# Turning the normalized rows of h with VectorE and small transfers instead of TensorE

## The chip, the cores and the metric

The kernel runs on one core of a Trainium2 chip. The metric is the device time of one execution in microseconds, and every comparison is between executions on the same chip. Engines are named as in the profile: PE (TensorE matmuls), PEld (its weight loads), DVE (VectorE), ACT (ScalarE), POOL (GpSimd) and SP (SyncE, which here only issues transfers).

## The reference

One transformer block on x of 2048 rows and 512 columns, float32: attention with 32 heads of 16, then a gated MLP whose gate mixes rows.

```python
q, k, v = split((layernorm(x) @ wqkv))           # 32 heads of 16
h = x + softmax(q k^T / 4) v @ wo                # 2048 x 512
z = gelu(layernorm(h) @ w_in)                    # 2048 x 1376
z1, z2 = z[:, :688], layernorm(z[:, 688:])
g = w_sp @ z2 + b_sp[:, None]                    # w_sp is 2048 x 2048
out = h + (z1 * g) @ w_out
```

## The kernel before

The program has four stages: projections of x; attention; a middle stage that turns each block of 128 rows of attention output into h, normalizes it and multiplies it into z; and the products with w_sp and w_out. Float32 operands of matmuls are split into a high and a low part (hi, lo), and a product is three matmuls (`mm3`, lines 108 to 110). The split is a copy by ACT into a rounded type (hi) and a subtraction by DVE (lo), line 100 and line 105.

The middle stage (lines 1000 to 1110) runs over 16 row blocks in the order of `h_rows`; step k finishes block `row[k]` and begins block `row[k + 3]`. PE, ACT, DVE, POOL and SP each work strictly in the order in which the program issues instructions there, so what stands behind a waiting instruction waits too. In step k:

- `make_h` (line 643): 12 matmuls of the split o with wo give h of `row[k + 3]`; DVE adds x (line 653), SP stores h to the scratch `h_scr` (line 655), and DVE takes its statistics (line 657) and computes mean and 1/std by small operations (lines 119 to 135).
- `turn` (line 1015): PE transposes the four 128x128 pieces of hn, the normalized block, of `row[k + 1]` into a PSUM tile, and ACT and DVE split them into hT.
- `make_z` on three groups of columns (464, 448, 464): 12 matmuls each, then gelu by ACT (line 1034). Between the first and the second group ACT and DVE split the o of `row[k + 4]` (`split_o`, lines 100 and 105, with the tile named o); after the second, DVE takes statistics of z (line 1094) and ACT writes hn of `row[k + 3]` (line 1097).
- `gate_z`: ACT's queue stores z (lines 1041 and 1047), ACT normalizes z2 (line 1046), and `load_o` fetches what `row[k + 5]` needs: o from its scratch (line 623), the reciprocal softmax sums rc, each row of which is read by 16 partitions (four transfers, line 626), and x (line 629). POOL then multiplies o by rc (line 630). In the second half POOL also forms sums of z for the next stage.

The last three steps make no h. The first three blocks are made at the end of attention (`more_h`, line 863): their matmuls stand among those of attention by the string FINAL, and DVE writes hn (line 883). The line 195 loads v in pieces of 128 bytes during attention; lines 285 and 677 are small transfers there.

Of the kernel before, what the change touches and what calls it, by code (L numbers as in the profile page):

```python
# [20 lines left out]
D = 512  # L21
# [5 lines left out]
NB = S // P  # L27
HB = NB // 2
NQ = S // 512
DB = D // P  # L30
# [30 lines left out]
def block_kernel(ctx: ExitStack, tc: tile.TileContext, x, wqkv, wo, w_in, w_sp4, b_sp, w_out, out):  # L61
# [7 lines left out]
    nc = tc.nc  # L69
# [20 lines left out]
    o_scr = dram.tile([D, S], F32, name="o_scr")  # L90
    r_scr = dram.tile([H, S], F32, name="r_scr")
    h_scr = dram.tile([S, D], F32, name="h_scr")
    z_scr = [dram.tile([S, FH], F32, name=f"z{i}_scr") for i in range(2)]
    s_scr = dram.tile([HB, P, HB, P], F32, name="s_scr")
    g_scr = [dram.tile([3, P, FC], F32, name=f"g{p}_scr") for p in range(HB)]

    def split(hi, lo, src, eh=None, el=None):

        if eh == "act":
            nc.scalar.activation(hi, src, AF.Copy)  # L100
        elif eh == "pool":
            nc.gpsimd.tensor_copy(hi, src)  # L102
        else:
            nc.vector.tensor_copy(hi, src)
        (nc.gpsimd if el == "pool" else nc.vector).tensor_sub(lo, src, hi.bitcast(F32))
# [508 lines left out]
    wi4 = w_in.rearrange("(a p) c -> p a c", p=P)  # L614

    h_rows = [0, 1, 2, HB, HB + 1, HB + 2] + [sb + HB * i for sb in range(3, HB) for i in range(2)]
    os_, o2s, xrs, hns, hTs = {}, {}, {}, {}, {}

    def load_o(sb):

        c = slice(sb * P, (sb + 1) * P)
        o = e2.tile([P, DB, P], F32, name="o")
        nc.sync.dma_start(o, o_scr[:, c].rearrange("(d p) s -> p d s", p=P))
        rc = e2.tile([P, DB, P], F32, name="rc")
        for d in range(DB):
            nc.sync.dma_start(rc[:, d, :], r_scr[8 * d:8 * d + 8, c].rearrange(
                "h (o s) -> h o s", o=1).to_broadcast([8, DH, P]))
        xrs[sb] = e2.tile([P, D], F32, name="xr", bufs=3)
        nc.sync.dma_start(xrs[sb], x[c, :])
        nc.gpsimd.tensor_mul(o, o, rc)  # L630
        os_[sb] = o
# [19 lines left out]
    def add_h(sb, acc, between=lambda: None):  # L651
        h = xrs[sb]
        nc.vector.tensor_add(h, acc, h)
        between()
        nc.sync.dma_start(h_scr[sb * P:(sb + 1) * P, :], h)
        hst[sb] = e2.tile([P, 6], F32, name="st")
        nc.vector.bn_stats(hst[sb], h)

    def scale_h(sb):
        mv = e2.tile([P, 2], F32, name="mv")  # L660
# [21 lines left out]
    with ExitStack() as at:  # L682
# [127 lines left out]
        def play_final(units):  # L810


            half = []
            for x in FINAL:
                if x == "G":
                    if not half:
                        unit = units.pop(0)
                        half.extend([unit, new_pt(), 0])
                        if unit[2] == 6 and sums_:
                            invert()  # L820
                        if len(units) in (7, 5):
                            load_o(h_rows[(7, 5).index(len(units)) + 3])
                    unit, pt, p = half
                    for step in score(unit, p, pt):
                        step()
                    half[2] += 1
                    if p:
                        waiting.append([(unit, pt, PLACES), 0])
                        half.clear()
                elif x == "V":  # L830
                    unit, *rest = waiting.pop(0)[0]
                    weigh(unit, *rest)
                    if unit[2] == NB - 1:
# [29 lines left out]
        def more_h(k):  # L863

            for _ in range(k):
                if not pieces:
                    sb = h_rows[len(hns)]
# [8 lines left out]
                after = h_rows[len(hns) + 1]  # L876
                o = os_.pop(after)
                hi, lo = o2s[after] = [e2.tile([P, DB, P], F32R, name=f"o2{i}", bufs=1) for i in range(2)]
                nc.vector.tensor_copy(hi, o)
                add_h(sb, acc, lambda: nc.vector.tensor_sub(lo, o, hi.bitcast(F32)))  # L880
                mv, rs = scale_h(sb)
                hns[sb] = e2.tile([P, D], F32, name="hn", bufs=3)
                nc.vector.tensor_scalar(hns[sb], xrs.pop(sb), mv[:, 0:1], rs,
                                        op0=ALU.subtract, op1=ALU.mult)

        made = [0]
        units = [(hg, qb, kb) for hg in range(HG) for qb in range(NQ) for kb in range(NB)]
# [3 lines left out]
        with tc.manual_schedule(engines={E.PE, E.Activation, E.DVE, E.SP}):  # L891
            end = len(units) - 2 * LEAD
            for n in range(0, end, 2):
                hg, qb, kb = units[n]
                if hg + 1 < HG and n % 64 < 24 and n % 4 == 0:
                    load_k(hg + 1, [n % 64 // 4])
                if hg + 1 < HG and n % 64 < 12 and n % 4 == 2:
                    load_d(hg + 1, [n % 64 // 4])
                if hg + 1 < HG and n % 64 == 30:
                    load_v(hg + 1)  # L900
                if kb == 2 and n // NB + 3 < HG * NQ:
                    load_q(n // NB + 3)
# [18 lines left out]
            load_o(h_rows[2])  # L921
            maxima.close()
# [77 lines left out]
    with ExitStack() as mid:  # L1000
        m2 = mid.enter_context(tc.tile_pool(name="mid_2", bufs=2))
        zs, zst = {}, {}
        hT = wc.tile([P, 2, 2, DB, P], F32R, name="hT", tag="w2")
        ph = mid.enter_context(tc.tile_pool(name="mid_ph", bufs=1, space=PSUM))
        pt = mid.enter_context(tc.tile_pool(name="mid_pt", bufs=2, space=PSUM))
        ps = mid.enter_context(tc.tile_pool(name="mid_ps", bufs=5, space=PSUM))

        turned = [0]

        def turn(sb):  # L1010

            hn = hns.pop(sb)
            tp = pt.tile([P, DB, P], F32, name="tp")
            for d in range(DB):
                nc.tensor.transpose(tp[:, d, :], hn[:, d * P:(d + 1) * P], ident)  # L1015
            hTs[sb] = [hT[:, i, turned[0] % 2] for i in range(2)]
            turned[0] += 1
            split(hTs[sb][0], hTs[sb][1], tp, "act")

        def new_z(sb):  # L1020
            zs[sb] = [m2.tile([P, FH], F32, name=f"z{i}", bufs=1 + 4 * i) for i in range(2)]
# [45 lines left out]

        w = [Slot(wc, f"w{i}") for i in range(3)]
        row = dict(enumerate(h_rows))
        turn(row[0])  # L1070
        for k in range(NB):
            sb, new = row[k], row.get(k + 3)
            if new is not None:
                make_h(new, (ph if k else ps).tile([P, 512], F32, name="acc"))
            if k + 1 < NB:
                turn(row[k + 1])
            if new is not None:
                mv, rs = scale_h(new)
                nb = minus_mean(e2, mv, rs)
# [13 lines left out]
            for c in range(2):  # L1093
                nc.vector.bn_stats(zst[sb][:, c, :], zs[sb][1][:, c * FC:(c + 1) * FC])
            if new is not None:
                hns[new] = e2.tile([P, D], F32, name="hn", bufs=3)
                nc.scalar.activation(hns[new], xrs.pop(new), AF.Identity, bias=nb, scale=rs)
            for c in chunks[2:]:
                make_z(sb, *c)
            hTs.pop(sb)  # L1100
# [358 lines left out]
```

## Time and profile before

| | |
|---|---|
| median of 3 runs | 1803.24 us (1802.75 to 1803.64) |
| profiled execution | 1802.38 us |
| its span in the profile | 1800.6 us |
| busy share of PE, DVE, ACT, POOL | 100%, 83%, 77%, 12% |
| middle stage | about 1351 to 1514 us |
| transfers of SP's queue | 143224 packets, 143.82 MB |

Rows of a timeline are start, duration (both us), engine, line, operation, output and input, and in brackets the engine's idle time before it with what ended it. SPq and ACTq are the queues of SP and ACT that issue transfers; the duration is that of the issue, not of the transfer. A row "x4" merges neighbours of one kind. Rows of a group have the median in the middle of three durations, in ns. The chain is the work that ended last, followed back from the end.

### The profile page before, as it was taken

The numbers are of one execution on the slowest core, as the hardware profiler recorded it, in microseconds if no ns is written. First come the engines' busy times: TensorE is split into PE (matmuls) and PEld (weight loads), VectorE is DVE, ScalarE is ACT, GpSimd is POOL, SyncE is SP. The second block draws the span as 40 slices with busy tenths as digits, with TensorE's granted clock in tenths as the row PEclk, the third lists the DMA queues.
The fourth block names the chain that finished last, engine by engine and source line by source line (L and its number), as shares of the span: only waits on it lengthen the run. The fifth ranks groups of instructions, "written<-read, shape, count | busy, mean of one in ns | idle before, by whom it ended". The sixth has DMA issues, their size and how long they took to land.

```text
span 1800.6 us, 36057 instructions
## 1 busy us (share of the span) xinstructions
PE 1793.1 (100%) x13371; PEld 1050.6 (58%) x13371; DVE 1500.0 (83%) x3034; ACT 1378.4 (77%) x2674; POOL 218.4 (12%) x299
## 2 busy tenths in 40 slices
PE   9999999999999999999999999999999999999999
PEld 6876444444444444444444444444448889999998
DVE  6487999999999999999999999999936676778664
ACT  3224999999999999999999999999994445334231
POOL 2241000011010100000000000000110754001111
PEclk9999999999999999999999999999999999999999
DMA  6677111221120111021012011100134554668562
GB/s 199 192 194 182 43 26 27 49 56 30 36 59 19 51 39 26 20 50 35 14 36 44 24 30 38 26 15 15 40 74 143 168 176 151 216 208 278 184 197 91
DMA packets 148184, 157.54 MB, mean 87 GB/s; under 512 B 63032, under 2 KB 93256, under 8 KB 146664
## 3 DMA queue, kind: packets, MB, share of 16 engines
q1 hardware_dynamic: 143224, 143.82, 29.6%
q10 hardware_dynamic: 4752, 11.41, 1.6%
q8 instruction: 105, 1.72, 0.4%
q14 instruction: 71, 0.58, 0.1%
q0 software_dynamic: 32, 0.01, 0.0%
HBM read 99.69 MB, written 54.56 MB: 86 GB/s over the span
## 4 chain that ended last, share of the span: by engine, by line
PE 99%; DVE 1%; DMA 0%; issue 0%; ACT 0%; DVEq 0%
PE pv L726 30%; PE s L700 10%; PE s L237 9%; PE m L700 9%; PE m L237 7%; PE acc L108 6%; PE acc L110 6%; PE acc L109 6%; PE g L110 4%; PE g L109 4%; PE g L108 4%; PE acc L643 2%; PE tp L1319 1%; PE h L643 1%; PE acc L1340 0%; PE tp L1015 0%
## 5 line engine op out<-in xcount | busy, mean ns | idle before, releaser
L704 ACT ACTIVATE pt<-s 128x512 f32<-128x512 f32 (+1 forms) x1149 | 668.5, 632 | 3.4 <-PE s L700 3.0
L726 PE MATMUL pv<-pt,vst 128*32 128x256 f32 (+1 forms) x6048 | 595.2, 467 | 0.0
L242 DVE TENSOR_REDUCE mx<-s 128x1 f32<-128x512 f32 x826 | 539.6, 682 | 42.3 <-PE s L237 34.4
L704 ACT ACTIVATE pt<-m 128x512 f32<-128x512 f32 x855 | 500.3, 616 | 0.2 <-PE m L700 0.2
L242 DVE TENSOR_REDUCE mx<-m 128x1 f32<-128x512 f32 x682 | 452.3, 682 | 28.3 <-PE m L237 21.2
L700 PE MATMUL s<-qst,kst 50*128 50x512 f32 x1193 | 418.5, 437 | 0.0
L237 PE MATMUL s<-kst,qst 48*128 48x512 f32 x963 | 343.7, 421 | 0.0
L700 PE MATMUL m<-qst,kst 50*128 50x512 f32 x855 | 340.1, 440 | 0.0
L237 PE MATMUL m<-kst,qst 48*128 48x512 f32 x794 | 290.8, 423 | 0.0
L700 PEld LDWEIGHTS s<-qst,kst 50*128 50x128 f32 x1193 | 187.4, 184 | 145.0 <-DVE mx L242 91.0
L726 PEld LDWEIGHTS pv<-pt,vst 128*32 128x32 f32 x6048 | 120.4, 108 | 217.6 <-issue 208.5
L700 PEld LDWEIGHTS m<-qst,kst 50*128 50x128 f32 x855 | 146.2, 184 | 129.4 <-DVE mx L242 88.9
L237 PEld LDWEIGHTS s<-kst,qst 48*128 48x128 f32 x963 | 166.8, 184 | 40.4 <-issue 12.8
L237 PEld LDWEIGHTS m<-kst,qst 48*128 48x128 f32 x794 | 137.1, 184 | 41.7 <-issue 15.2
L247 ACT ACTIVATE ab<-s 128x512 f32<-128x512 f32 x167 | 100.4, 601 | 14.2
L102 POOL CAST mparts<-nm 128x16 fp32r<-128x16 f32 x32 | 6.3, 196 | 861.3 <-DVE nm L255 861.3
L251 DVE CUSTOM_DVE_ANT_0 ab<-s,ab 128x512 f32<-128x512 f32 x137 | 93.2, 680 | 5.1 <-PE s L237 5.1
L955 ACT ACTIVATE ws<-a 128x512 fp32r<-128x512 f32 x80 | 45.7, 621 | 48.7 <-PE g L110 23.8
L251 DVE CUSTOM_DVE_ANT_0 ab<-m,ab 128x512 f32<-128x512 f32 x112 | 76.2, 680 | 4.9 <-PE m L237 4.9
L237 PE MATMUL s<-dst,qst 48*128 48x512 f32 x167 | 79.6, 477 | 0.0
L1034 ACT ACTIVATE z<-acc 128x464 f32<-128x464 f32 (+2 forms) x64 | 27.5, 456 | 63.5 <-PE acc L110 63.5
L108 PE MATMUL acc<-wi,hT 128*128 128x464 f32 (+2 forms) x196 | 72.8, 371 | 0.0
(219 smaller groups left out, 2586.9 us busy)
## 6 DMA issues: line engine op xcount, KB each, us to landing
a<-in_w_sp SPq DMA_DIRECT2D x80, 256.0 KB
qst<-q_scr SPq DMA_DIRECT2D x192, 64.0 KB
z_scr<-z ACTq DMA_DIRECT2D x32, 344.0 KB
kst<-k_scr SPq DMA_DIRECT2D x42, 256.0 KB
k_scr<-part SPq DMA_DIRECT2D x16, 512.0 KB
q_scr<-part SPq DMA_DIRECT2D x16, 512.0 KB
z<-z_scr SPq DMA_DIRECT2D x14, 344.0 KB
b<-z_scr SPq DMA_DIRECT2D x24, 172.0 KB
```

The source lines that it names most:

```text
L108: nc.tensor.matmul(ps, lh, rh, start=first, stop=False)
L109: nc.tensor.matmul(ps, lh, rl, start=False, stop=False)
L110: nc.tensor.matmul(ps, ll, rh, start=False, stop=last)
L237: nc.tensor.matmul(acc, q[r, p, c], keys[r, p], start=True, stop=True)
L242: nc.vector.reduce_max(at(t, e if t else e - 1), acc, axis=AX.X)
L247: nc.scalar.activation(ab[0], acc, AF.Relu)
L251: nc.vector.tensor_tensor_reduce(ab[0], acc, ab[0], 1.0, LOW, ALU.add, ALU.max, at(0, 0))
L643: yield nc.tensor.matmul(acc, o2[b][:, d, :], wo2[a][:, d, :], start=i == 0, stop=i == 3 * DB - 1)
L700: nc.tensor.matmul(out, kst[hg % 2][r, p, kb * P:(kb + 1) * P], qst[hg * NQ + qb][r, p, :], start=True, stop=True)
L704: nc.scalar.activation(out, scores, AF.Exp, scale=DH ** -0.5)
L726: nc.tensor.matmul(pv[0][32 * j:32 * j + 32, cols], vst[hg % 2][:, c:c + 32], pt[:, places[t, p], cols], start=kb == 0, stop=kb == NB - 1 ...
L955: nc.scalar.activation(hi, src, AF.Copy)
```

## The change

The transposes of hn by PE go, with the PSUM tile they used. Instead, as soon as hn is written, `flip` has DVE transpose the block in 32x32 squares, each in its place, and four transfers of SP (512 pieces of 128 bytes each) carry the squares to their transposed places in a new scratch in DRAM, `ht_scr`. A step later `fetch_turned` loads the turned block (256 KB) from there, and a step after that `split_turned` has ACT and DVE split it, now from SBUF. The first block is fetched and split during the end of attention, by DVE alone, and the second is fetched there.

```diff
+    def flip(sb, hn):
+        z = e2.tile([P, D], F32, name="hz", tag="hn", bufs=3)
+        nc.vector.transpose(z, hn)
+        q = 32
+        for i in range(P // q):
+            c = sb * P + q * i
+            nc.sync.dma_start(ht_scr[:, c:c + q].rearrange("(j r) c -> r j c", r=q),
+                              z[q * i:q * i + q, :].rearrange("r (j c) -> r j c", c=q))
+
+    def fetch_turned(sb, pool, **slot):
+        raws[sb] = pool.tile([P, DB, P], F32, name="ht", **slot)
+        nc.sync.dma_start(raws[sb], ht_scr[:, sb * P:(sb + 1) * P].rearrange("(a p) s -> p a s", p=P))
+
+    def split_turned(sb, eh=None):
+        hTs[sb] = [hT[0][:, i, turns[0] % 2] for i in range(2)]
+        turns[0] += 1
+        split(hTs[sb][0], hTs[sb][1], raws.pop(sb), eh)
...
@@ play_final, more_h: the end of attention
+                        if len(units) in (13, 3):
+                            fetch_turned(h_rows[(13, 3).index(len(units))], e2, tag="rc")
...
+                if made[0] == 6 * DB:
+                    split_turned(h_rows[0])
...
+                flip(sb, hn)
@@ the middle stage
-        pt = mid.enter_context(tc.tile_pool(name="mid_pt", bufs=2, space=PSUM))
-        ps = mid.enter_context(tc.tile_pool(name="mid_ps", bufs=5, space=PSUM))
-        def turn(sb):
-            hn = hns.pop(sb)
-            tp = pt.tile([P, DB, P], F32, name="tp")
-            for d in range(DB):
-                nc.tensor.transpose(tp[:, d, :], hn[:, d * P:(d + 1) * P], ident)
...
-            split(hTs[sb][0], hTs[sb][1], tp, "act")
+        ps = mid.enter_context(tc.tile_pool(name="mid_ps", bufs=7, space=PSUM))
...
-        turn(row[0])
         for k in range(NB):
...
             if k + 1 < NB:
-                turn(row[k + 1])
+                split_turned(row[k + 1], "act")
+            if k + 2 < NB:
+                fetch_turned(row[k + 2], m2)
...
             if new is not None:
-                hns[new] = e2.tile([P, D], F32, name="hn", bufs=3)
-                nc.scalar.activation(hns[new], xrs.pop(new), AF.Identity, bias=nb, scale=rs)
+                hn = e2.tile([P, D], F32, name="hn", bufs=3)
+                nc.scalar.activation(hn, xrs.pop(new), AF.Identity, bias=nb, scale=rs)
+                flip(new, hn)
             for c in chunks[2:]:
                 make_z(sb, *c)
             hTs.pop(sb)
             gate_z(sb, lambda: k + 5 < NB and load_o(row[k + 5]))
```

SP in one step of the middle stage, before, from one store of h to the next (xr holds h here, and then x of a later block):

```order
L655 DMA h_scr<-xr 128x512
L623 DMA o<-o_scr 128x4x128
L626 DMA rc<-r_scr 128x1x128 x4
L629 DMA xr<-in_x 128x512
L655 DMA h_scr<-xr 128x512
```

and after (lines 656, 624, 627 and 630 are the old 655, 623, 626 and 629):

```order
L656 DMA h_scr<-xr 128x512
L673 DMA ht<-ht_scr 128x4x128
L667 DMA ht_scr<-hz 32x16x32 x4
L624 DMA o<-o_scr 128x4x128
L627 DMA rc<-r_scr 128x1x128 x4
L630 DMA xr<-in_x 128x512
L656 DMA h_scr<-xr 128x512
```

The load of a turned block and the four transfers to the scratch now stand between the store of h and the six transfers of load_o.

DVE in the same step, before, around the statistics of z (o is the low part of the split o):

```order
L666 TENSOR_SCALAR nb<-rs_r_19272,mv 128x1
L105 TENSOR_TENSOR o_19294<-o,o_19293 128x512
L1094 BN_STATS zst<-z_19277 128x6 x2
L1043 BN_AGGR zmv<-zst 128x2
L119 TENSOR_SCALAR rs_v_19333<-zmv 128x1
```

and after:

```order
L690 TENSOR_SCALAR nb<-rs_r_19287,mv 128x1
L106 TENSOR_TENSOR o_19309<-o,o_19308 128x512
L1111 BN_STATS zst<-z_19292 128x6 x2
L663 STREAM_TRANSPOSE hz<-hn 128x512
L1059 BN_AGGR zmv<-zst 128x2
L120 TENSOR_SCALAR rs_v_19354<-zmv 128x1
```

The transpose stands behind the statistics of z and ahead of the operations that make its mean and 1/std. ACT's order is as it was, but for the source of the split into hT.

More of the change, by code (lines that the diff above doesn't have):

```diff
@@ L92, in block_kernel @@
     h_scr = dram.tile([S, D], F32, name="h_scr")
+    ht_scr = dram.tile([D, S], F32, name="ht_scr")
     z_scr = [dram.tile([S, FH], F32, name=f"z{i}_scr") for i in range(2)]
@@ L616, in block_kernel @@
     h_rows = [0, 1, 2, HB, HB + 1, HB + 2] + [sb + HB * i for sb in range(3, HB) for i in range(2)]
-    os_, o2s, xrs, hns, hTs = {}, {}, {}, {}, {}
+    os_, o2s, xrs, hTs = {}, {}, {}, {}
     def load_o(sb):
@@ L657, in add_h @@
         nc.vector.bn_stats(hst[sb], h)
+    def flip(sb, hn):
[13 more added lines that the diff above has]
+        split(hTs[sb][0], hTs[sb][1], raws.pop(sb), eh)
+    raws, turns, hT = {}, [0], []
     def scale_h(sb):
@@ L866, in more_h @@
                 if not pieces:
-                    sb = h_rows[len(hns)]
+                    sb = h_rows[made[0] // (3 * DB)]
                     acc = later[0].tile([P, 512], F32, name="h")
@@ L875, in more_h @@
                 pieces.clear()
-                after = h_rows[len(hns) + 1]
+                if made[0] == 6 * DB:
+                    split_turned(h_rows[0])
+                after = h_rows[made[0] // (3 * DB)]
                 o = os_.pop(after)
@@ L881, in more_h @@
                 mv, rs = scale_h(sb)
-                hns[sb] = e2.tile([P, D], F32, name="hn", bufs=3)
-                nc.vector.tensor_scalar(hns[sb], xrs.pop(sb), mv[:, 0:1], rs,
+                hn = e2.tile([P, D], F32, name="hn", bufs=3)
+                nc.vector.tensor_scalar(hn, xrs.pop(sb), mv[:, 0:1], rs,
                                         op0=ALU.subtract, op1=ALU.mult)
+                flip(sb, hn)
         made = [0]
@@ L921, in block_kernel @@
             load_o(h_rows[2])
+            hT.append(wc.tile([P, 2, 2, DB, P], F32R, name="hT", tag="w2"))
             maxima.close()
@@ L1095, in block_kernel @@
             if new is not None:
-                hns[new] = e2.tile([P, D], F32, name="hn", bufs=3)
-                nc.scalar.activation(hns[new], xrs.pop(new), AF.Identity, bias=nb, scale=rs)
+                hn = e2.tile([P, D], F32, name="hn", bufs=3)
+                nc.scalar.activation(hn, xrs.pop(new), AF.Identity, bias=nb, scale=rs)
+                flip(new, hn)
             for c in chunks[2:]:
```

4 lines of the change are left out of this document (removed).

## Prediction

> **What bounds the kernel now.** I read the page first, then stretches of the stage that turns hn into z (about 1351 to 1514 us), then the chain through that stage, then the waits.
>
> ```profile
> PE 1793.1 (100%) x13371; PEld 1050.6 (58%) x13371; DVE 1500.0 (83%) x3034; ACT 1378.4 (77%) x2674; POOL 218.4 (12%) x299
> PEclk9999999999999999999999999999999999999999
> ```
>
> PE has no idle time worth the name and the granted clock is full in every slice, so time can only be won by giving PE less, and is lost as soon as PE waits. The stretches of the stage (busy us of PE, PEld, DVE, ACT, POOL; then clock, DMA share, GB/s), with the end of attention first:
>
> ```profile
> 1300.00:1351.00 51.00, 50.98 (x362) 20.72 (x358) 20.42 (x57) 47.86 (x58) 5.82 (x6) 1.00 0.29 67
> 1362.00:1426.00 64.00, 64.00 (x314) 56.34 (x313) 44.75 (x146) 27.14 (x48) 32.02 (x37) 1.00 0.57 170
> 1426.00:1512.00 86.00, 86.00 (x432) 76.75 (x431) 55.91 (x180) 37.25 (x67) 55.98 (x65) 1.00 0.53 166
> ```
>
> PE is busy for all of it; ACT has half its time free, DVE a third, the DMA engines over 40%. Now the chain over the stage, and over one step of its loop:
>
> ```profile
> by line: PE acc L110 24.4%; PE acc L109 24.3%; PE acc L108 24.3%; PE acc L643 22.0%; PE tp L1015 4.4%; PE pv L726 0.3%; PE g L108 0.2%; PE g L110 0.2%; PE g L109 0.2%
> ```
> ```profile
> 1383.99 2.76 PE acc L643 x12
> 1386.75 0.44 PE tp L1015 x4
> ```
> ```profile
> 1351.36 0.59 PE tp L1015 x4
> ...
> 1394.66 2.77 PE acc L643 x12
> ```
>
> The chain is PE alone. A step with an h takes 1394.66 - 1383.99 = 10.67 us; the turning by TensorE that the change removes is 0.44 us of it (0.59 for the first), and 4.4% of 163.7 us = 7.2 us in all. That is the whole prize: without it a step is 10.23 us.
>
> **The change part by part.** *Removed:* 64 transposes, 7.2 us of PE, all of it on the chain. ACT and DVE split as many elements as before, from SBUF instead of PSUM: nothing, they have room.
>
> *Added:* per row block one 128x512 transpose on DVE, four transfers of 512 pieces of 128 bytes on SP, and one load of the turned block. What matters is where they stand. On SP the four transfers stand ahead of the six transfers of load_o, and they wait for hn, which ACT makes only after its split of o in the same step. Load_o fetches the o that ACT splits in the next step. So a ring closes: split of o, two gelus, hn (ACT), transpose (DVE), four transfers, load_o (SP), landing, o times rc (POOL), the next split of o. One turn of the ring is one step. In the kernel before, load_o stood right behind the store of h, early in the step, and no such ring existed:
>
> ```profile
> 1387.51 0.33 SPq L655 DMA_DIRECT2D h_scr<-xr  x1
> 1387.93 0.39 SPq L623 DMA_DIRECT2D o<-o_scr  x1
> 1388.37 2.47 SPq L626 DMA_DIRECT2D rc<-r_scr  x4
> ...
> 1390.94 0.39 SPq L629 DMA_DIRECT2D xr<-in_x  x1
> ```
>
> Its time round is a sum of rows. ACT and DVE first, in step 0, where nothing waits between them:
>
> ```profile
> 1359.52 0.62 ACT L100 ACTIVATE o<-o 128x512 fp32r<-128x512 f32 x1
> 1360.17 0.61 ACT L1034 ACTIVATE z<-acc 128x224 f32<-128x224 f32 x2
> 1360.66 0.82 ACT L1097 ACTIVATE hn<-xr,nb,rs_r 128x512 f32<-128x512 f32 x1
> ```
> ```profile
> 1346.76 0.43 DVE L879 CAST o<-o 128x512 fp32r<-128x512 f32 x1 [7.72 <-PE h L643]
> ...
> 1350.99 0.55 DVE L883 TENSOR_SCALAR hn<-xr,mv,rs_r 128x512 f32<-128x512 f32 x1
> ...
> 1360.18 0.69 DVE L105 TENSOR_TENSOR o<-o,o 128x512 fp32r<-128x512 f32 x1 [1.32 <-ACT o L100]
> 1360.79 0.93 DVE L1094 BATCH_NORM_STATS2 zst<-z 128x6 f32<-128x344 f32 x2
> ```
> ```profile
> L281 DVE STREAM_TRANSPOSE mturned<-mparts x32: 199/204/211, 142.7 to 1307.2; 128x32 f32<-128x32 f32 x32
> ```
>
> Hn ends 1360.66 + 0.82 - 1359.52 = 1.96 us after the split of o starts, but DVE, which has the transpose behind the statistics of z, is free at 1360.79 + 0.93 - 1359.52 = **2.20**. The only transpose in the trace has 32 columns (0.20 us); for 512 columns the other operations of that shape take 0.43 to 0.69. I take **0.7**, with 0.43 below and 1.1 (twice 0.55) above.
>
> Then SP's issuing, and how long load_o takes to be usable:
>
> ```profile
> 1304.82 0.38 SPq L623 DMA_DIRECT2D o<-o_scr  x1
> ...
> 1327.99 1.70 SPq L677 DMA_DIRECT2D r_scr<-rcp  x4
> ...
> 1368.13 0.47 SPq L623 DMA_DIRECT2D o<-o_scr  x1
> ```
> ```profile
> L285 SPq DMA_DIRECT2D qst<-mturned x256: 610/610/1058, 143.0 to 1313.4; - x128
> ```
> ```profile
> 1312.64 1.29 POOL L630 TENSOR_TENSOR o<-o,rc 128x512 f32<-128x512 f32 x1 [5.48 <-DMA rc<-r_scr]
> ...
> 1377.81 1.29 POOL L630 TENSOR_TENSOR o<-o,rc 128x512 f32<-128x512 f32 x1 [8.69 <-DMA rc<-r_scr]
> ...
> 1396.52 1.28 POOL L630 TENSOR_TENSOR o<-o,rc 128x512 f32<-128x512 f32 x1 [9.46 <-DMA rc<-r_scr]
> ```
>
> Four small transfers in a row cost SP 1.70 us (r_scr) to 4 x 0.61 = 2.44 (mturned): **2.1**. From the issue of load_o's first transfer to POOL's start on it: 1396.52 - 1387.93 = 8.59 in a mid step, 1377.81 - 1368.13 = 9.68 in another, and 1312.64 - 1304.82 = 7.82 at the end of attention, before any z or h store adds traffic. So it is the load's own time, not a queue: **8.6**. POOL's product: **1.3**. Sum: 2.2 + 0.7 + 2.1 + 8.6 + 1.3, and 0.1 for the handing over, is **15.0 us** a turn, against 10.23 that PE would need. The ring, not PE, sets the step.
>
> What the 2048 new packets of a step take on the DMA engines is not in the trace as a write. The nearest row is the load of v, which moves 4096 pieces of 128 bytes:
>
> ```profile
> 236.59 2.18 SPq L195 DMA_DIRECT2D raw<-v_scr  x2
> ```
> ```profile
> 237.00:242.00 5.00, 5.00 (x43) 2.35 (x43) 4.68 (x10) 4.95 (x12) 0.00 (x0) 1.00 0.73 110
> ```
>
> 0.73 x 5.0 us x 16 engines / 4096 = 14 ns a piece, so 2048 take 1.8 us of all engines. They pass while SP issues (2.1 us), so I add 0; at worst load_o queues behind all 1.8. Ends of the turn: 2.20 + 0.43 + 1.70 + 7.82 + 1.28 = 13.4 below, 2.20 + 1.1 + 2.44 + 9.68 + 1.29 + 1.8 = 18.5 above. [...]
>
> *How the ring adds up.* Load_o runs in steps 0 to 10, so there are 11 turns between the split of o in step 0 and in step 11:
>
> ```profile
> 1475.62 0.62 ACT L100 ACTIVATE o<-o 128x512 fp32r<-128x512 f32 x1
> ```
> ```profile
> 1476.27 0.69 DVE L105 TENSOR_TENSOR o<-o,o 128x512 fp32r<-128x512 f32 x1
> ```
> ```profile
> 1479.91 2.93 PE L643 MATMUL acc<-wo,o 128*128 128x512 f32 x12
> ```
>
> The first split moves up by the two turnings ahead of it, 0.59 + 0.44: 1359.52 - 1.03 = 1358.5. Eleven turns of 15.0 put the last at 1523.5 (now 1475.62). Both halves of o are ready 1476.27 + 0.69 - 1475.62 = 1.34 later; PE starts the last h at 1524.8 instead of 1479.91: 44.9 late. After it three turnings are still saved, 3 x 0.44 = 1.3. Net **+43.6 us**. Break-even is a turn of 11.0 us: 1358.5 + 11 x 11.03 + 1.34 - 1.3 is 1479.9.
>
> *What I cost at nothing.* The three blocks turned during attention: DVE is busy for 20 of 51 us there, SP's later transfers move by 2.1 us, and r_scr, written last, is read steps later. The DVE transpose delays the statistics chain of z by 0.7 us; ACT waits there with nothing due. The loads of turned blocks are issued a step before they are split. For the last one the time is shortest:
>
> ```profile
> 1482.84 0.44 PE tp L1015 x4
> ...
> 1490.76 0.44 PE tp L1015 x4
> ```
>
> Steps without h take 7.92 - 0.44 = 7.5 us, so from hn in step 12 (some 9 us into it) to its product in step 15 there are 10.2 + 7.5 + 7.5 - 9 = 16 us, for 0.7 + 2.1 and twice a landing of up to 5: covered by 3 us; it would show only if both landings took over 6.6.
>
> Idle PE of 15.0 - 10.2 = 4.8 us a step is new; the trace, at full clock throughout, cannot show what follows an idle. [...]
>
> **The rivals.**
> *The ring is hidden, and PE's saving is all that shows.* If load_o were usable 3.8 us after its issue, a turn would be 10.2 and PE would stay the bound: 1802.4 - 7.2 = 1795.2. For it: in mid steps the load shares the engines with stores, so its 8.6 us could shrink at the new place. Against it: 7.82 at a quiet time. The decision falls at a turn of 10.23.
> *The load is quicker, but not by that much.* At a turn near 11.0 nothing changes: 1802. It needs the load in 4.6 us.
> *The small writes are dear.* If each of the 2048 packets took what the mean packet of SP's queue takes,
>
> ```profile
> q1 hardware_dynamic: 143224, 143.82, 29.6%
> ```
>
> 0.296 x 1800.6 us x 16 / 143224 = 59.5 ns, a block needs 128 x 59.5 ns = 7.6 us on each engine; load_o queues behind 7.6 - 2.1 = 5.5 of it, a turn is 20.5, and the kernel takes 1846 + 11 x 5.5 = 1906.5. For it: they are scattered writes to DRAM. Against it: 14 ns apiece in reads of the same size. [...]
>
> **How the numbers follow.** The profiled execution took 1802.38 us (its span 1800.6), 0.05% under the median of the runs, 1803.24; sums are against it, and a shift of 0.9 is within what I can tell. A measurement can tell about 0.2% (3.6 us) from no change. Forecast 1802.4 + 43.6 = **1846.0**, chance 0.82, from 1828.7 (turn 13.4) to 1884.6 (turn 18.5). Hidden ring 0.07 (1795.2), no change 0.03, dear writes 0.08 (1906.5). Since the five terms will not all be at one end, 1827 to 1878 holds 8 in 10. Faster 0.07, same 0.03, slower 0.90.
>
> **What would show it.** Right: no TensorE transposes in this stage; PE idle before L643 in steps 1 to 12, ended by the split of o; ACT's split of o waiting for POOL, POOL for rc; SP waiting for the transpose ahead of the four transfers; h stores about 15 us apart, then steps of 10.2 and 7.5. Wrong: h stores 10.2 us apart, or PE waiting for the turned block's split (then the round trip through the scratch is the bound), or load_o landing in under 5 us.

## The result, and the profile after

| | before | after |
|---|---|---|
| median of 6 runs | 1802.95 us (1802.62 to 1803.64) | 1861.73 us (1858.83 to 1863.08) |
| ratio | | 1.0323 [1.0310, 1.0336] |
| profiled execution | 1802.38 us | 1859.43 us |
| its span | 1800.6 us | 1857.6 us |

The changed kernel is 3.2% slower. First PE and its granted clock on the page, and the middle stage in the two stretches shown of before (busy us of PE, PEld, DVE, ACT, POOL; then clock, DMA share, GB/s):

```profile
PE 1807.0 (97%) x13307; PEld 1053.1 (57%) x13307; DVE 1513.7 (81%) x3051; ACT 1376.9 (74%) x2673; POOL 221.5 (12%) x299
PEclk9999999999999999999999999999998899999999
```
```profile
1362.00:1426.00 64.00, 47.59 (x196) 39.09 (x197) 33.12 (x105) 20.96 (x39) 7.39 (x7) 0.89 0.53 147
1426.00:1512.00 86.00, 69.16 (x282) 57.28 (x282) 46.03 (x147) 24.06 (x43) 42.86 (x51) 0.88 0.57 149
```

PE, busy for all of both stretches before, is now idle for 16 of 64 us and 17 of 86, and the clock, full before, is at 0.88 to 0.89. No other engine got busier: something waits, nothing is overloaded. The waits of the stage (engine, line, what it waited for: total us, times, longest) name the chain:

```profile
POOL o L631 <- DMA rc<-r_scr: 102.2, 11, 14.8
ACT o L101 <- POOL o L631: 79.3, 11, 8.6
PE acc L644 <- ACT o L101: 42.4, 12, 5.2
```

PE waits for ACT's split of o, ACT for POOL's product, POOL for the reciprocal sums. One turn, on the chain from one split of o to the next (which began at 1393.94 and begins again at 1408.05):

```profile
1396.14 0.61 DVE hz L663
...
1397.15 0.54 SPq L667
...
1399.10 0.45 SPq L624
1399.60 0.59 SPq L627
...
1401.48 5.15 DMA rc<-r_scr
...
1406.75 1.27 POOL o L631
...
1408.05 0.64 ACT o L101
```

This is the ring of the prediction: transpose, four transfers, load_o, landing, product, split. It is 14.11 us here. ACT's first operations of the stage, and its last split of o:

```profile
1361.48 1.28 ACT L1050 ACT_TABLE_LOAD   x1 [8.07 <-DMA sums<-o]
...
1363.23 0.62 ACT L101 ACTIVATE o<-o 128x512 fp32r<-128x512 f32 x1
```
```profile
1533.43 0.63 ACT L101 ACTIVATE o<-o 128x512 fp32r<-128x512 f32 x1 [8.15 <-POOL o L631]
```

Eleven turns lie between, so a mean turn is (1533.43 - 1363.23) / 11 = 15.47 us, against 15.0 forecast. PE's first matmuls of an h in a mid step, of the last h, and the first product with w_sp:

```profile
1394.62 4.73 PE L644 MATMUL acc<-wo,o 128*128 128x512 f32 x12 [5.24 <-ACT o L101]
```
```profile
1534.12 1.55 PE L644 MATMUL acc<-wo,o 128*128 128x512 f32 x3 [4.49 <-ACT o L101]
```
```profile
1569.57 0.40 PE L109 MATMUL g<-t,ws 128*128 128x344 f32 x1 [0.59 <-POOL t L986]
```

The last h starts 54.2 us later than before (1479.91), and the execution ends 57.05 us later (1859.43 - 1802.38). The first split of o is only 3.7 us later than before (1363.23 against 1359.52), so 50.5 us of the loss lie inside the ring.

### The profile page after: what moved, and what is told of

The parts are those of the page before. It is cut to its first block, busy times and chain, and to the rows that moved or that the text cites. A ratio compares the mean times of both kernels' runs of the same rounds, so it can differ in the third digit from the quotient of the medians.

```text
span 1857.6 us, 36087 instructions
## 1 busy us (share of the span) xinstructions
PE 1807.0 (97%) x13307; PEld 1053.1 (57%) x13307; DVE 1513.7 (81%) x3051; ACT 1376.9 (74%) x2673; POOL 221.5 (12%) x299
## 4 chain that ended last, share of the span: by engine, by line
PE 87%; DMA 5%; DVE 3%; SPq 3%; ACT 1%; POOL 1%; issue 1%; POOLq 0%; ACTq 0%; DVEq 0%
PE pv L750 29%; PE s L724 10%; PE s L238 9%; PE m L724 8%; PE m L238 7%; PE g L111 4%; PE g L110 4%; PE g L109 4%; DMA rc<-r_scr 4%; PE acc L109 3%; PE acc L111 3%; PE acc L110 3%; SPq L667 1%; SPq L627 1%; POOL o L631 1%
## 5 line engine op out<-in xcount | busy, mean ns | idle before, releaser
L248 ACT ACTIVATE ab<-s 128x512 f32<-128x512 f32 x167 | 100.5, 602 | 14.1
L644 PE MATMUL acc<-wo,o 128*128 128x512 f32 x156 | 55.2, 514 | 42.5 <-ACT o L101 42.4
```

The costliest lines, as they stand in the source:

```text
L248: nc.scalar.activation(ab[0], acc, AF.Relu)
L644: yield nc.tensor.matmul(acc, o2[b][:, d, :], wo2[a][:, d, :], start=i == 0, stop=i == 3 * DB - 1)
```

## The experiments

The theory from the profile: the four transfers stand ahead of load_o on SP and close a ring; without that the change would cost nothing. Rivals: the 128-byte pieces are dear in themselves; or the load's landing is set by other traffic. Each ratio below is to the kernel before on the same chip.

**The prize alone.** The kernel before without the transposes of PE:

```diff
...
-            tp = pt.tile([P, DB, P], F32, name="tp")
-            for d in range(DB):
-                nc.tensor.transpose(tp[:, d, :], hn[:, d * P:(d + 1) * P], ident)
+            tp = hn.rearrange("p (d s) -> p d s", d=DB)
```

> The kernel before with the transposes by TensorE left out: hn is split into hT as it stands, so h is not turned and z is of other numbers. It measures the prize alone. All theories: 7.2 us of PE's chain go, 1795 to 1797 us. If PE's own time were not the bound of the stage, 1800 or more.

Measured: 1797.88 us (1797.35 to 1798.94), ratio 0.9971 [0.9960, 0.9982]. What PE can give back is about 5 us, a little less than the 7.2 read off the chain.

**One store ahead of load_o.** No small piece anywhere, the kernel before with one plain store of hn on SP:

```diff
...
                 nc.scalar.activation(hns[new], xrs.pop(new), AF.Identity, bias=nb, scale=rs)
+                nc.sync.dma_start(hn_scr[new * P:(new + 1) * P, :], hns[new])
```

> The kernel before, turning by TensorE, with one plain store of hn (256 KB in rows of 2 KB, to a scratch that nobody reads) issued on SP ahead of load_o. No small pieces, no transpose on DVE, no round trip. Theory (ring): the wait of that one transfer for hn closes the same ring with a shorter turn: 1.96 (split to hn) + 0.5 (issue) + 7.7 to 8.6 (load_o) + 1.3 (POOL) + 0.1 = 11.6 to 12.5 us against a step of 10.67, so 1811 to 1822 us. Rivals 1 and 2: nothing of theirs is in it, 1803 to 1805 us.

Measured: 1832.10 us (1829.56 to 1835.89), ratio 1.0163 [1.0146, 1.0180]; a turn of 13.31 us. SP's and ACT's waits of this kernel between 1362 and 1512 us:

```profile
SPq L1099 <- ACT hn L1098: 81.4, 11, 8.7
```
```profile
ACT o L101 <- POOL o L631: 55.3, 11, 6.3
```

A single plain store costs 1.6% when it waits for hn ahead of load_o. The ring needs neither small pieces nor VectorE. It costs more than I expected because load_o, started there, took 9.2 to 10.3 us to reach POOL.

**Large pieces.** The changed kernel, the same four transfers, in pieces of 512 bytes:

```diff
-            c = sb * P + q * i
-            nc.sync.dma_start(ht_scr[:, c:c + q].rearrange("(j r) c -> r j c", r=q),
-                              z[q * i:q * i + q, :].rearrange("r (j c) -> r j c", c=q))
+            c = sb * P
+            nc.sync.dma_start(ht_scr[P * i:P * i + P, c:c + P].rearrange("(r j) c -> r j c", j=DB),
+                              z[q * i:q * i + q, :].rearrange("r (j c) -> r j c", c=P))
```

> The changed kernel with the same four transfers, same bytes and same place in SP's order, but in 512 pieces of 512 bytes a block instead of 2048 of 128 bytes; the squares are then not put in their places, so the block isn't turned. Theory (ring): SP still issues four transfers ahead of load_o, so the turn loses at most what load_o queues behind small packets, 0 to 1.8 us of 15.5: 1840 to 1862 us. Rival 1 (small packets): most of the loss goes, under 1815 us.

Measured: 1874.90 us (1872.62 to 1875.82), ratio 1.0395 [1.0379, 1.0410]; a turn of 16.91 us. Four times fewer pieces are not faster but slower (after's ratio is 1.0323), above the theory's range and far from the rival's. The four issues took 2.5 to 2.8 us and the load 10.1 on average (8.7 to 10.9), both more than after; together they are the 1.4 us a turn. Why the load took longer is open. SP's queue on the pages of after and of this kernel (packets, MB, share of 16 engines):

```profile
q1 hardware_dynamic: 185464, 152.22, 30.9%
```
```profile
q1 hardware_dynamic: 160888, 152.22, 30.6%
```

After's packets take 0.309 x 1857.6 = 574.0 us of all 16 engines, this kernel's 0.306 x 1873.3 = 573.2, before's 0.296 x 1800.6 = 533.0. So the four transfers and the loads of turned blocks add 41 us over 16 blocks, 2.6 us a block, whichever the pieces; over after's 42240 added packets that is 16 ns each. The rival of dear small writes (59.5 ns) falls.

**Twice the transfers ahead of load_o.** The changed kernel, each block written to a second scratch as well:

```diff
...
+        for scr in (ht_scr, hu_scr):
-        for i in range(P // q):
+            for i in range(P // q):
...
-            nc.sync.dma_start(ht_scr[:, c:c + q]...
+                nc.sync.dma_start(scr[:, c:c + q]...
```

> The changed kernel with the four transfers issued twice, the second time to a scratch that nothing reads, both ahead of load_o. Theory (load_o pays for the issue of what stands ahead of it, 2.2 us for four): a turn is 15.5 + 2.2 = 17.7 us, 11 turns make 24 us more: 1882 to 1892. Rival A (what costs is the pieces themselves on the DMA engines, 2048 more a step): the load also lands later, a turn grows by 4 us or more and the time is above 1905. Rival B (the issue is hidden, the load's landing is set by something else): 1860 to 1868.

Measured: 1911.07 us (1909.52 to 1912.61), ratio 1.0599 [1.0583, 1.0615]; a turn of 19.07, 3.6 us more than after. That is above the theory's range; the time is in rival A's, though the turn grew by less than the 4 us that rival A asked for. SP in one turn of this kernel:

```profile
1406.45 2.31 SPq L669 DMA_DIRECT2D ht_scr<-hz  x4
1408.81 2.80 SPq L669 DMA_DIRECT2D hu_scr<-hz  x4
1411.70 0.66 SPq L625 DMA_DIRECT2D o<-o_scr  x1
```

The second four hold load_o for 2.9 us, not 2.2, and the load then takes 9.7 us to POOL (average of 11) instead of 9.0: 2.9 + 0.7 is the 3.6 found. Both theories had a part; most of it is the issue. Eleven turns make 40 of the 51 us between the two profiled executions; 3 lie ahead of the first split of o and 8 behind the last, and why is open. The run also prices the pieces by themselves: SP's queue took 0.320 x 1908.7 = 610.8 us of all 16 engines, 36.8 more than after's, for 33792 further packets, or 17 ns each.

**The transfers behind the load.** The changed kernel with the four transfers issued after load_o (SP: store of h, load of the turned block, load_o, four transfers):

```diff
...
-                flip(new, hn)
+                move = flip(new, hn)
...
             gate_z(sb, lambda: k + 5 < NB and load_o(row[k + 5]))
+            if new is not None:
+                move()
```

> The changed kernel, with the four transfers to the scratch issued behind load_o in each step of the middle stage; the transpose on DVE, the pieces and their number are as they were. Theory (the ring through SP's order): the ring is open, PE sets the step at about 10.2 us, and the time is 1794 to 1802 us; ACT's split of o no longer waits for POOL. Rival 1 (the 2048 small packets of a block burden the DMA engines): the packets are the same, so 1840 us or more. Rival 2 (the round trip through the scratch, or DVE's added work, is late for PE): 1840 us or more, since the transfers go out later still.

Measured: 1834.56 us (1832.90 to 1838.76), ratio 1.0177 [1.0162, 1.0192]; a turn of 12.76. No range held it: the theory said 1794 to 1802, the rivals 1840 or more. Of the 63.9 us between the changed kernel and the one without turning, this order gives back 27.2. The prediction's ring is open, but another wait closed a new one. SP's waits and the chain of this kernel:

```profile
SPq L627 <- DMA z_scr<-z: 25.1, 8, 4.0
```
```profile
1403.55 3.50 DMA z_scr<-z
...
1407.06 0.57 SPq L627
...
1407.68 7.07 DMA rc<-r_scr
```

The third transfer of rc waits 3.5 us for a store of z, which it has nothing to do with. The instruction list of the program says why: SP's and ACT's transfers take eight completion counters in turn, and a transfer waits until the one that last had its counter has landed. With 14 transfers a step instead of 9, the transfer eight places ahead is a store of z of the same step.

**load_o first.** The changed kernel with load_o right behind the store of h, its old place:

```diff
                 make_h(new, (ph if k else ps).tile([P, 512], F32, name="acc"))
+            if k + 5 < NB:
+                load_o(row[k + 5])
...
-            gate_z(sb, lambda: k + 5 < NB and load_o(row[k + 5]))
+            gate_z(sb, lambda: None)
```

> The changed kernel with load_o issued right behind the store of h, ahead of the load of the turned block and of the four transfers, as it stood before the change. Theory (the ring through SP's order is all that was lost): the load goes out some 10 us earlier, POOL's product is done well ahead of ACT's split, PE has no idle time in steps 1 to 12 beyond what the kernel before had, and the time is that of the kernel without any turning, 1797.9, plus up to 4: 1796 to 1804, faster than the kernel before by 0 to 0.4%. Second theory (from the run with the moves behind the load): a transfer of SP that shares a completion slot with a store of z waits for that store; here it would be the store of h, which stands ahead of load_o, so load_o goes out late in part of the steps: 1800 to 1815, with waits of SP on z_scr<-z. Rival (the small writes or their traffic are themselves dear, wherever they stand): PE still waits for o in each step and the time stays above 1820.

Measured: 1842.69 us (1841.12 to 1843.43), ratio 1.0218 [1.0203, 1.0234]; a turn of 13.41. None of the three fits as a whole. The second named the wait that came, but on another transfer, and priced it too low. The rival's time came and PE still waits for o, but not because o lands late: POOL's product is now always in time, and the split behind it is late. SP's, ACT's and PE's waits, and the chain:

```profile
SPq L630 <- DMA z_scr<-z: 48.9, 8, 7.5
```
```profile
ACT hT L101 <- DMA ht<-ht_scr: 52.6, 11, 6.5
```
```profile
PE acc L644 <- DVE o L106: 18.0, 10, 2.5
```
```profile
1407.24 4.11 DMA z_scr<-z
...
1411.85 3.69 DMA ht<-ht_scr
```

Now it is load_o's own last transfer, of x, that shares a counter with a store of z; in the instruction lists, of SP and of ACT:

```
L630 DMA xr<-in_x 128x512 [waits DMAHW2_49,Activation_49]
L1057 DMA z_scr<-z_19557 128x688 [waits DMAHW2_49,Activation_49]
```

Behind it on SP stands the load of the turned block, whose split is the first thing ACT and DVE do in the next step. The ring runs through z instead of o. In the first two steps SP waited for no store of z; there the load of the turned block was issued right behind load_o's six transfers and took 8.46 and 8.31 us to land, against 3.0 to 4.5 in the nine steps behind such a wait:

```profile
1364.92 8.46 DMA ht<-ht_scr
```

**The same, twice the transfers.** This was to show that pieces off the ring cost nothing:

```diff
...
+        for scr in (ht_scr, hu_scr):
...
+                nc.sync.dma_start(scr[:, c:c + q]...
```

> As the run with load_o right behind the store of h, but with the four transfers issued twice (2048 further pieces of 128 bytes a step, to a scratch that nothing reads). Theory (the transfers cost by their place ahead of load_o, not by their pieces): the second set costs nothing, within 4 us of that run. Rival (small pieces load the DMA engines so that the loads land late): 10 us or more above it.

Measured: 1902.92 us (1900.47 to 1905.55), ratio 1.0554 [1.0538, 1.0570], 60 us above the run before it. My theory missed widely, though not for the rival's reason alone: the waits of SP show load_o itself held by stores of z, since 18 transfers a step now share the eight counters.

```profile
SPq L628 <- DMA z_scr<-z: 30.7, 7, 6.0
```

**The late first split.** The changed kernel with the four transfers of the last block of attention held until the last gather has been issued:

```diff
...
-                flip(sb, hn)
+                move = flip(sb, hn)
+                if sb == h_rows[2]:
+                    held.append(move)
+                else:
+                    move()
...
             play_final(units[end:])
+            held.pop()()
```

> The changed kernel with the four transfers of the last block made in attention (row 2) issued behind the last gather's transfers instead of ahead of them. If the late first split (1363.2 instead of 1358.5) comes from those four transfers alone, the ring starts 4.7 us earlier: 1857. If it comes mostly from ACT's new wait for the gather's last landing (the first tile of z lies where the gathered o lay), only the 1.5 to 2 us by which the gather's transfers move up come back: 1859.5 to 1861. If the first split does not matter to the end: 1861.7.

Measured: 1861.68 us (1861.34 to 1862.57), ratio 1.0326 [1.0309, 1.0343]: no change.

```profile
1361.15 1.28 ACT L1059 ACT_TABLE_LOAD   x1 [6.48 <-DMA sums<-o]
...
1362.89 0.62 ACT L101 ACTIVATE o<-o 128x512 fp32r<-128x512 f32 x1
```

ACT's wait is 1.6 us shorter, but the gather began later, and the split moved by only 0.3 us. So the transfers' place is not what delays it; the new wait is. In the list of the changed kernel this instruction waits for all eight counters, in that of before for PE alone; with the profile's name for the wait, that says that the first tile of z came to lie in memory that the last gather still reads. That the layout alone costs the 4.7 us was not tried apart.

**Stores of z on POOL's queue, moves behind the load.** The stores then have counters of their own:

```diff
...
-            nc.scalar.dma_start(z_scr[0][rows, :], z[0])
+            nc.gpsimd.dma_start(z_scr[0][rows, :], z[0])
...
-            nc.scalar.dma_start(z_scr[1][rows, :], z[1])
+            nc.gpsimd.dma_start(z_scr[1][rows, :], z[1])
```

> As the run with the moves behind load_o (SP: store of h, load of the turned block, load_o, four transfers), but with the two stores of z issued by POOL's queue, whose transfers have completion slots of their own, instead of ACT's. Theory (what held that run, and the one with load_o first, is that a load on SP shares a slot with a store of z and waits for it): no wait of SP on z_scr<-z is left, the ring is open, and the time is near that of the kernel without turning, 1798 to 1806. Second outcome: POOL waits for z ahead of its product o times rc, which then comes late: 1806 to 1825, with ACT's split of o waiting for POOL. Rival (the small writes or loads are slow in themselves): PE still waits each step with the loads landing late, 1830 or more.

Measured: 1833.11 us (1831.57 to 1835.32), ratio 1.0165 [1.0148, 1.0182]; a turn of 12.52. Its waits on stores of z are gone from SP, as the theory said, and yet the time is nearly that of the moves behind the load, in the rival's range: SP now waits for the pieces themselves, and holds the four transfers for counters of load_o.

```profile
SPq L677 <- DMA ht_scr<-hz: 20.2, 25, 2.1
```
```profile
1407.38 5.81 SPq L669 DMA_DIRECT2D ht_scr<-hz  x4
1413.29 0.92 SPq L656 DMA_DIRECT2D h_scr<-xr  x1
1416.93 0.38 SPq L677 DMA_DIRECT2D ht<-ht_scr  x1
```

The four take 5.81 us to issue instead of 2.2 (in the instruction list the last two share counters with transfers of load_o), the load of the turned block then starts 3 us behind the store of h, once the last pieces have landed, and load_o stands behind it. POOL is a second bound: in the steps in which it forms sums, the product, the sums and the issue of the two stores follow each other without a gap and take 12.6 us (1426.69 to 1439.29).

**The four transfers on POOL's queue.** SP's order is then that of before plus the load of the turned block:

```diff
-            nc.sync.dma_start(ht_scr[:, c:c + q].rearrange("(j r) c -> r j c", r=q),
+            nc.gpsimd.dma_start(ht_scr[:, c:c + q].rearrange("(j r) c -> r j c", r=q),
```

> The changed kernel with the four transfers of each block issued by POOL's queue instead of SP's; SP's order is then that of the kernel before plus the load of the turned block. Theory (it is SP's order that lost the time): load_o leaves early again, and if POOL needs up to 1.5 us for each issue, 6 us a step, its product is still in time: 1798 to 1808. Second outcome: POOL needs over 2.5 us for a transfer of 512 pieces, is held 10 us or more a step, and its product o times rc comes late: 1820 or more, with PE waiting for POOL. Rival (the writes are dear on the DMA engines): load_o lands late although it is issued early, 1820 or more with POOL waiting for rc.

Measured: 1831.44 us (1829.16 to 1832.85), ratio 1.0155 [1.0140, 1.0170]; a turn of 12.76, above the theory's range. The load of the turned block still stands ahead of load_o and waits for the pieces, 27 times, up to 9.0 us:

```profile
SPq L673 <- DMA ht_scr<-hz: 68.4, 27, 9.0
```

POOL issues the four transfers in 2.6 us, less than the theory allowed, but where it also forms sums it has no room for them. From one product to the next it is never idle there:

```profile
1420.54 1.27 POOL L631 TENSOR_TENSOR o<-o,rc 128x512 f32<-128x512 f32 x1
...
1432.01 2.60 POOL L667 DMA_DIRECT2D ht_scr<-hz  x4
1434.62 1.30 POOL L631 TENSOR_TENSOR o<-o,rc 128x512 f32<-128x512 f32 x1
```

That is 14.08 us: 1.3 for the product, 10.2 for the sums, 2.6 for the issue. Five of the ten steps from product to product take 14.1 us in this way, and from 1407.68 to 1448.77 the chain is POOL alone. In the kernel before, product and sums took 11.3 us there (1396.52 to 1407.83), already more than a step of PE.

**load_o first, stores of z on POOL's queue.** Both edits from above together.

> As the run with load_o right behind the store of h (SP: store of h, load_o, load of the turned block, four transfers), but with the two stores of z issued by POOL's queue. Theory: two things held the earlier runs, a wait of SP for a landed store of z (load_o first, stores of z on ACT's queue) and the load of the turned block ahead of load_o waiting for its pieces to land (moves behind the load, z on POOL); here neither stands ahead of load_o, so no ring closes inside a step: 1797 to 1806. Second outcome: SP still waits for a transfer of load_o that shares a slot with one of the four (the third and fourth moves come 8 issues behind the rc transfers), which delays the load of the turned block and ACT's split of it in part of the steps: 1806 to 1825. Rival (the pieces or loads are slow in themselves wherever they stand): 1830 or more.

Measured: 1828.12 us (1826.69 to 1829.67), ratio 1.0139 [1.0122, 1.0156]; a turn of 11.86. It lies between the second outcome and the rival. A wait of ACT, the second stretch, and one link of the chain:

```profile
ACT z L1050 <- DMA z_scr<-z: 26.1, 10, 5.2
```
```profile
1426.00:1512.00 86.00, 79.67 (x348) 68.56 (x349) 63.00 (x187) 32.81 (x60) 59.26 (x76) 0.94 0.74 192
```
```profile
1401.09 7.89 DMA ht<-ht_scr
```

POOL now issues the stores of z behind its product, so the one buffer of that half of z comes free late. The DMA engines are at 0.74. The load of a turned block, issued right behind load_o again, takes 7.89 us, as in the first two steps of the run with load_o first.

**Both remedies for the order.** load_o first, the four transfers on POOL's queue, POOL's product behind them:

```diff
...
-            nc.sync.dma_start(ht_scr[:, c:c + q].rearrange("(j r) c -> r j c", r=q),
+            nc.gpsimd.dma_start(ht_scr[:, c:c + q].rearrange("(j r) c -> r j c", r=q),
...
+                mul = load_o(row[k + 5], True)
...
-            gate_z(sb, lambda: k + 5 < NB and load_o(row[k + 5]))
+            gate_z(sb, lambda: k + 5 < NB and mul())
```

> The four transfers issued by POOL's queue, and load_o's transfers right behind the store of h on SP, ahead of the load of the turned block; POOL's product o times rc behind the four transfers and ahead of its sums. Theory (the time is lost where a load that POOL and ACT need soon stands on a queue behind a transfer that waits: for hn, for a landed store of z, for landed pieces): nothing that waits stands ahead of load_o any more, the load of the turned block has some 2 us to spare, and the time is 1797 to 1806. Second outcome: POOL, with 9 us of sums in every second step, issues the transfers late, the load of the turned block waits for them and ACT's split of it with all behind it: 1806 to 1825. Rival (the small pieces slow the loads wherever they stand): load_o needs over 10 us again although nothing on SP waits, 1825 or more.

Measured: 1822.05 us (1821.23 to 1823.09), ratio 1.0104 [1.0087, 1.0121], the second outcome and the best with blocks turned this way; a turn of 11.98. What is left is spread over many waits:

```profile
1362.00:1426.00 64.00, 56.64 (x252) 47.55 (x251) 42.80 (x137) 24.11 (x45) 33.53 (x42) 0.97 0.68 182
1426.00:1512.00 86.00, 78.70 (x354) 67.88 (x353) 59.34 (x178) 32.78 (x59) 71.24 (x92) 0.96 0.71 201
```
```profile
SPq L679 <- DMA ht_scr<-hz: 27.6, 11, 7.2
```
```profile
ACT hT L101 <- DMA ht<-ht_scr: 26.4, 9, 6.5
```

The load of the turned block, behind load_o, took 7.9 to 11.0 us in the three places where it is on the chain, and POOL's product, sums and four issues took 14.5 us without a gap, on the chain (1434.20 to 1448.68).

## Why the prediction was right, and where it was off

**The bound and the prize.** PE bounded before, and PE's waits are the whole loss. The prize was 5.1 us where 7.2 was forecast (its interval reaches from 3.2 to 7.2). Without turning, the stage takes 156.6 us from its first matmul (1352.81) to the first product with w_sp (1509.39), against 162.7 before (1351.29 to 1513.97): 6.1 us less. Against that, attention ended 1.5 us later; why is open.

**The ring.** Right in each link and in its sign: undoing the order gives back 19 to 40 us, by where the transfers go instead, and a plain store in the same place costs 29 us without any of the rest. The terms of a turn, forecast and measured:

| | forecast | measured |
|---|---|---|
| split of o to transpose | 2.20 | 2.12 (1393.94 to 1396.06) |
| transpose | 0.7 | 0.69 |
| four issues, with handing over | 2.2 | 2.3 |
| load_o to POOL | 8.6 | 9.0 (7.65 to 9.76, 11 turns) |
| POOL to split | 1.3 | 1.3 |
| turn | 15.0 | 15.47 |

The one term that was mis-sized is the load: 0.4 of the 0.47 us that a turn was forecast too short, 5.2 us over eleven turns. The forecast had taken 8.6, the lower of its two rows from mid steps (8.59 and 9.68).

**Where 13.4 us were missing.** Forecast +43.6, measured +57.05. The turns are 5.2 of it. The first split was forecast at 1358.5 and came at 1363.23: 4.7. This is the step "what I cost at nothing", the blocks turned during attention; it failed by a wait that the forecast did not have, ACT's first gelu behind the last gather. From the last split to PE took 0.69 instead of 1.34, as PE starts on the high half alone: -0.65. From the last h to the first product with w_sp takes 35.45 us where before took 34.06, so instead of saving 1.3 it lost 1.4: 2.7. A last 1.45 us lies behind the stage, its cause open.

**The clock.** The trace of before could not show what follows an idle PE. After does: behind an idle of 5.24 us the twelve matmuls of an h take 4.73 us, and the granted clock is 0.50 from 1394.6 to 1397.6; in before they take 2.93 at full clock. The restart costs 4.73 - 2.93 = 1.8 us here, which the forecast's sum had at nothing. The length of the idle alone does not decide it: in after an idle of 3.19 us left PE at full clock (1.00 from 1502.1 to 1506.1, the twelve matmuls in 3.29 us). In the run with load_o first, idles of nearly the same length went both ways:

```profile
1389.00 0.73 PE L644 MATMUL acc<-wo,o 128*128 128x512 f32 x2 [1.46 <-ACT o L101]
1391.44 3.92 PE L644 MATMUL acc<-wo,o 128*128 128x512 f32 x10 [1.71 <-DVE o L106]
...
1404.12 0.73 PE L644 MATMUL acc<-wo,o 128*128 128x512 f32 x2 [1.29 <-ACT o L101]
1406.57 2.56 PE L644 MATMUL acc<-wo,o 128*128 128x512 f32 x10 [1.71 <-DVE o L106]
```

The first ten matmuls took 3.92 us and the second ten 2.56. What decides between the two is open. Inside the ring a slow restart costs nothing, since PE has slack there (idle for 16 of 64 us); the last one (4.88 us against 2.93) is part of the 2.7 above.

**The rivals.** The hidden ring falls with the measured load, 9.0 us where it needed 3.8. The dear writes fall with 16 to 17 ns a packet where they needed 59.5; the forecast had 14, from reads. The run with pieces of 512 bytes speaks against them too: it was no faster (1874.90 us, after 1861.73), and SP's queue took 573.2 us of all 16 engines where after took 574.0.

**What my theory of the cause missed.** Before the experiments I held that the order on SP was all that was lost. It was the first bound of several. Each of the other orders took away the wait that it aimed at and shortened the turn, from 15.47 us to between 13.41 and 11.86; then another bound held. It was a counter shared with a store of z, the pieces' landing ahead of the load of the turned block, POOL's own 12.6 to 14.5 us in steps with sums when POOL also issues transfers, or the landing of the turned block behind load_o. Beside these stands the amount of transfers. The DMA share times the turn is the work of a step on all 16 engines: before 0.55 x 10.55 = 5.8 us, after 0.55 x 15.47 = 8.5, in the last run 0.70 x 11.98 = 8.4; the difference is about the 2.6 us a block counted above. At PE's 10.2 us a step this would be a share of 0.82; the two stretches of the stage reached 0.77 at most in any run. That this amount is a bound is not shown. Nor is it shown that the landing of the turned block follows the share: in the run with load_o first it took 8.46 us (from 1364.92) and 3.69 us (from 1411.85) in one stretch, whose share is 0.61. What differs between the two is whether load_o's six transfers had been issued just ahead; that was not tried apart. Whether an order exists that reaches 10.2 us stays open. No version with blocks turned in this way beat the kernel before; only the kernel without turning did, by 5 us.

## What to carry to other kernels

Before a transfer is put on a queue, look for what stands behind it there and ask whether the transfer's own input depends on that by way of the other engines: if so, a step costs the sum round that ring, whatever the engines' shares say (15.47 us here, with PE idle for 16 of 64). Taking one of several near-equal waits away gains only the distance to the next (here the turn went from 15.47 us to no less than 11.86), so find that distance before counting the gain. Before an issue is moved to another engine's queue, add up what that engine does in the same step, sums included. And count a step's transfers, not only their bytes: with eight completion counters, as in this program, a fast transfer can wait for a slow one that it has nothing to do with (a transfer of rc for a store of z, 3.5 us).

## What the hardware showed that I had not expected

- load_o's transfer of x on SP waited up to 7.5 us for a store of z issued by ACT (load_o first), because the program gives both queues the same eight completion counters.
- Pieces of 128 and of 512 bytes cost the DMA engines the same for the same bytes: with them SP's queue took 574.0 and 573.2 us of all 16 engines, 41 and 40 more than before.
- Behind an idle of 1.69 us in the run with one store ahead PE took 4.72 us for the twelve matmuls of an h, about as long as behind 5.24 us in after (4.73, with a clock of 0.50 for the first 3 us); behind 3.19 us in after the clock stayed at 1.00 and they took 3.29.
- POOL issues four transfers of 512 pieces in 2.60 us, SP in 2.2.
- DVE transposes 128x512 float32 in 32x32 squares in 0.69 us, as long as its subtraction of that size.
